# Early loads of an attention and MLP kernel, each issued when the load three places ahead has landed

## The chip, the cores and the metric

One core of a Trainium2 chip runs the whole program. The metric is the device time of one execution in microseconds (us), the median of several runs. The engines are called PE (matrix multiply, with PEld for its weight loads), DVE, ACT and POOL (elementwise engines) and SP, whose queue issues nearly all transfers. A transfer is cut over the core's 16 DMA engines and counts as landed when all its parts are there.

## What is computed

First linear attention for 8 batches of 8 heads, 576 positions and head size 64; then an MLP without activation, whose weights arrive as 64-bit floats. Cut to what matters:

```python
def phi(x):                                   # q and k, scaled by D ** -0.25
    h = x @ omega.T - (x * x).sum(-1, keepdims=True) / 2
    return exp(h - h.max(-1, keepdims=True)) / sqrt(128)
kv, z = k_p.T @ v, k_p.sum(over positions)    # per batch and head
attn  = (q_p @ kv) / (q_p @ z + 1e-6)
x     = attn as (4608, 512)
out   = ((x @ w_a) * (x @ w_b)) @ w_out       # 512 -> 1536 -> 512
```

## The kernel before

The work is a graph of about 5,000 operations. Attention goes by units (one batch, two heads): `pair` does the first ones, `shifted` the later ones; the MLP follows by batches in `moe_block` and `moe_block7`. Every matmul operand in the MLP is split into a high and a low part, so weights are converted on the chip (ACT lines 452 and 454, DVE line 456, then lines 398 and 404). The order in which the operations are emitted is a list written out by hand (`ORDER`), and the buffer slot of each tile is another one (`SLOTS`), so each engine's instruction order is fixed. The change alters neither.

A transfer is emitted by the helper `dma` (line 406), which issues on SP's queue at line 407. SP does these in order: an instruction that waits holds up all transfers behind it. A few transfers are issued elsewhere (ACT's queue brings `om`, line 428; line 960 spreads `qd`), none of them on SP's queue in the first 42 us.

The first transfers that `dma` issues, numbered from 0 as the change numbers them, with their KB:

```
 0 X   256   1 X   256   2 ident 64   3 Xe    256   4 X    512   5 nat   512
 6 X   512   7 v   330   8 nat  512   9 X     512  10 v    330  11 nat   512
12 raw 512  13 raw 512  14 raw  512  15 v     330  16 raw  512  17 raw   512
18 raw 512  19 natee 256 20 natk 256 21 v     330  22 v    330  23 X     512
24 raw 512  25 raw 512  26 natq 256  27 raw   512  28 natkk 256 29 raw   512
30 raw 512  31 natk 256
```

X holds q and k of a unit, from which PE makes the scores (line 587); nat, natee, natk and natq hold the same rows the other way round, for the sums of squares (POOL line 750, ACT lines 749 and 566, then DVE lines 752 and 571); v goes to the PE bursts of line 1040; raw is a block of 64-bit weights. Loads 0 and 1 are unit 0's X, 4, 6 and 9 those of units 1 to 3; 5, 8 and 11 are the nat of units 1 to 3; 7, 10, 15 and 21 the v of units 0 to 3; 22 and 23 belong to unit 4.

Of the kernel before, what the change touches and what calls it, by code (L numbers as in the profile page):

```python
# [196 lines left out]
    at=(  # L197
        "0123456705613412652106537451673260731742751346507163014510110101010101101010100101011010101001010101101001010101010101010101010110101010101010101010101010010101"
        "01010101010101010101010101010101010101010101"),
# [23 lines left out]
    a="101010101010101010101010",  # L223
# [132 lines left out]
def tile_attention_moe(ctx: ExitStack, tc: tile.TileContext, kqt, kqtt, kqn, kqnt, vx, omst, idn, wab, wout, out):  # L356
    nc = tc.nc
# [7 lines left out]
    def f(ap):  # L365
        return ap.bitcast(F32)

    g = Graph()
    for name, n in dict(X=2, Xw=0, natw=0, nat=2, x2=0, v=2, hk=1, hq=2, qd=1, kvz=0, sm=3, sq=3, ht=3, Xt=1, xl=0, xts=2, rd=2, x=4, xa=2, xf=2, Sa=2, Sb=2, st=0,
                        w=NF, u=NF, t=0, tst=0, wo=3, raw=2, a=2, c=0, bq=0, ghl=2, osb=0, ot=0, owr=0, og=0, ogf=0, oc=0, zs=1, z2=1, zb=2, k2=2, kl=1, dn=1, tails=0, zq=2, zx=2,  # L370
                        at=CFG["AT"], ab=2, o=4).items():
# [31 lines left out]
    def subber(o, i, hi):  # L403
        return lambda e: ENG[e].tensor_tensor(o(), i(), f(hi()), op=ALU.subtract)

    def dma(dst, src):
        return lambda e: nc.sync.dma_start(dst(), src())


    ident = fixed([P, P], F32, "ident")  # L410
# [20 lines left out]
    if CFG["IDSP"]:  # L431
        g.op({"SP": 450}, dma(lambda: ident.ap[:], lambda: idn), w=[(ident, None)], prio=-1396.5, nbytes=65536)
    else:
        g.op({"ACT": 60}, lambda e: nc.scalar.dma_start(ident.ap[:], idn), w=[(ident, None)], prio=-5000, nbytes=65536)
# [35 lines left out]
    for n, (kind, i, w) in enumerate(units):  # L470
        pr = 4000 + n * 4000 / len(units)
        more = late[:10] if n < 18 else late[:6] if n < 24 else late[:3] if n < 30 else late[:1] if n < 33 else []
        raw = g.buf("raw", [P, NW], I64 if wide else F32, f"raw{n}", more)
        src = (wab[i, w] if kind == "ab" else wout[i])
        g.op({"SP": 450}, dma(lambda raw=raw: raw.ap[:], lambda src=src: src), w=[(raw, None)], alloc=[raw], prio=pr - 600,
             nbytes=P * NW * (8 if wide else 4))
        if kind == "ab":
            hb = wab_b[i, w] = g.buf("wu"[i % 2], [P, 2, NC4, P], F32R, f"w{'ab'[w]}{i}")
            v = lambda hb, k: hb.ap[:, k].rearrange("p c f -> p (c f)")
        else:  # L480
            hb = wo_b[i] = g.buf("wo", [P, 2, E], F32R, f"wo{i}")
            v = lambda hb, k: hb.ap[:, k]
        convert(raw, lambda hb=hb, v=v: v(hb, 0), lambda hb=hb, v=v: v(hb, 1), hb, NW, pr, CFG["CONV"][0] + n * CFG["CONV"][1], n < NF)
        if kind == "o":
            db = g.buf(None, None, None, f"wod{i}")
            wo_store[i] = db
            g.op({"SP": 450}, dma(lambda i=i: wod[i], lambda hb=hb: f(hb.ap)), r=[(hb, None)], w=[(db, None)], prio=pr + 600,
                 nbytes=P * 2 * E * 4)
# [1143 lines left out]
```

## Time and profile before

| | us |
|---|---|
| median of 3 runs | 1031.1 (1031.01, 1031.1, 1032.39) |
| the profiled execution's own time | 1031.69 |
| its span, first to last instruction | 1029.7 |
| PE busy in the span | 1021.7 (99%) |
| DVE busy | 789.8 (77%) |
| ACT busy | 637.8 (62%) |

The span is what the views below divide; some 2 us lie around it. The mean granted TensorE clock is 0.999. All transfers together move 312.95 MB, 304 GB/s on average.

### The profile page before, as it was taken

What the parts mean: (1) busy time and instruction counts of PE and PEld (TensorE: products, weight loads), DVE (VectorE), ACT (ScalarE), POOL (GpSimd) and SP (SyncE); (2) the same over time, 40 slices, a digit from 0 to 9 for tenths busy, and PEclk for the clock granted to TensorE, in tenths of its full rate; (3) what the DMA queues carried; (4) which work ended last, traced back from release to release, by engine and by line L of the source; (5) the groups of instructions that cost most, each with busy time, mean ns of one, the idle gap of its engine ahead of it and who ended that gap; (6) DMA issues with size and microseconds to landing.
All of it is one profiled execution on the core that took longest, in us unless ns stands there. A gap on an engine that the chain in (4) does not pass through costs nothing.

```text
span 1029.7 us, 25658 instructions
## 1 busy us (share of the span) xinstructions
PE 1021.7 (99%) x9963; PEld 900.4 (87%) x9963; DVE 789.8 (77%) x1561; ACT 637.8 (62%) x1688; POOL 110.8 (11%) x182
## 2 busy tenths in 40 slices
PE   9999999999999999999999999999999999999998
PEld 7777777778788889888889988888888999999998
DVE  7999999999987877776767767687756467877555
ACT  7999998776676666675666556675654134344322
POOL 2012111210111111111110011111110000000000
PEclk9999999999999999999999999999999999999999
DMA  9787888998999999989898998989797888989981
GB/s 355 244 308 255 274 257 281 328 320 285 338 338 321 340 350 333 341 299 324 286 341 306 325 290 284 350 273 320 242 331 244 307 281 329 366 319 346 358 310 60
DMA packets 122185, 312.95 MB, mean 304 GB/s; under 512 B 17488, under 2 KB 39120, under 8 KB 122064
## 3 DMA queue, kind: packets, MB, share of 16 engines
q1 hardware_dynamic: 121600, 310.72, 87.6%
q8 instruction: 79, 1.29, 0.5%
q10 hardware_dynamic: 464, 0.59, 0.2%
q14 instruction: 42, 0.34, 0.1%
HBM read 254.74 MB, written 56.52 MB: 302 GB/s over the span
## 4 chain that ended last, share of the span: by engine, by line
PE 96%; DVE 3%; ACT 0%; issue 0%; DVEq 0%; ACTq 0%
PE p L1405 41%; PE o L1120 23%; PE pb L1307 6%; PE pa L1307 6%; PE o_P L1190 5%; PE pkv L906 3%; PE pm L977 2%; PE ppk L607 2%; PE ppk L587 2%; PE p L607 1%; PE p L1190 1%; DVE sm L659 1%; PE ppke L587 1%; DVE raw L456 0%; PE none L426 0%; DVE sq L752 0%
## 5 line engine op out<-in xcount | busy, mean ns | idle before, releaser
L1120 PE MATMUL o<-wo,ghl 128*128 128x512 f32 x1008 | 269.6, 397 | 0.0
L1120 PEld LDWEIGHTS o<-wo,ghl 128*128 128x128 f32 x1008 | 178.6, 188 | 35.5 <-issue 4.3
L396 ACT COPY c<-p 128x512 f32<-128x512 f32 x150 | 87.5, 583 | 182.0 <-PE p L1405 174.4
L1417 DVE TENSOR_TENSOR c<-p,c 128x512 f32<-128x512 f32 x144 | 98.7, 685 | 63.8 <-PE p L1405 36.5
L1405 PE MATMUL p<-Sa,t 128*128 128x256 f32 x1008 | 133.9, 282 | 0.0
L1405 PEld LDWEIGHTS p<-Sa,t 128*128 128x128 f32 x1008 | 126.9, 190 | 2.4 <-issue 0.3
L859 POOL TENSOR_TENSOR z<-hk 128x256 f32<-128x256 f32 x54 | 47.2, 873 | 610.5 <-ACT hk L627 356.1
L1481 DVE TENSOR_TENSOR c<-c 128x512 f32<-128x512 f32 x82 | 56.7, 696 | 46.3 <-ACT c L396 45.7
L1307 PE MATMUL pa<-x,wa 128*128 128x512 f32 x288 | 79.6, 400 | 0.0
L941 ACT ACTIVATE hq<-hq,dn 128x128 f32<-128x128 f32 x216 | 70.5, 393 | 11.9 <-DVE dn L937 11.5
L1307 PE MATMUL pb<-x,wb 128*128 128x512 f32 x288 | 77.8, 397 | 0.0
L1405 PE MATMUL p<-x,wb 128*128 128x256 f32 x504 | 73.5, 281 | 0.0
L1405 PE MATMUL p<-x,wa 128*128 128x256 f32 x504 | 73.4, 281 | 0.0
L1405 PEld LDWEIGHTS p<-x,wa 128*128 128x128 f32 x504 | 67.7, 189 | 2.9
L1405 PE MATMUL p<-Sb,bq 128*128 128x256 f32 x504 | 67.7, 283 | 0.0
L1405 PE MATMUL p<-x,t 128*128 128x256 f32 x504 | 67.5, 282 | 0.0
L1405 PEld LDWEIGHTS p<-Sb,bq 128*128 128x128 f32 x504 | 64.9, 189 | 2.9
L1405 PEld LDWEIGHTS p<-x,t 128*128 128x128 f32 x504 | 64.7, 189 | 2.9
L1405 PE MATMUL p<-Sb,t 128*128 128x256 f32 x504 | 67.0, 282 | 0.0
L1405 PEld LDWEIGHTS p<-x,wb 128*128 128x128 f32 x504 | 65.6, 189 | 0.1
L1405 PEld LDWEIGHTS p<-Sb,t 128*128 128x128 f32 x504 | 63.4, 189 | 1.4 <-ACT c L396 0.5
L1307 PEld LDWEIGHTS pb<-x,wb 128*128 128x128 f32 x288 | 53.3, 188 | 12.7 <-issue 0.9
(225 smaller groups left out, 1969.2 us busy)
## 6 DMA issues: line engine op xcount, KB each, us to landing
t<-td SPq DMA_DIRECT2D x168, 512.0 KB
wo<-wod SPq DMA_DIRECT2D x96, 512.0 KB
bq<-bd SPq DMA_DIRECT2D x84, 256.0 KB
qdr<-qd SPq DMA_DIRECT2D x108, 160.0 KB
hq<-qdr SPq DMA_DIRECT2D x27, 640.0 KB
X<-in_kqt_dram SPq DMA_DIRECT2D x30, 512.0 KB
raw<-in_wab_dram SPq DMA_DIRECT2D x24, 512.0 KB
td<-ts SPq DMA_DIRECT2D x24, 512.0 KB
```

The lines of the kernel that those rows point to most:

```text
L396: nc.scalar.copy(o(), i())
L587: nc.tensor.matmul(pps[w].ap[half, c * M:c * M + M], x()[rows, c * P + D * t:c * P + D * t + D], mo.ap[rows], start=True, stop=True)
L607: nc.tensor.matmul(flat[c // 4][w]()[half, c % 4 * M:c % 4 * M + M], x()[rows, c * P + D * t:c * P + D * t + D], om.ap[rows], start=True, ...
L859: g.op({"POOL": pool2(n)}, lambda e: nc.gpsimd.tensor_tensor(o(), a(), c(), op=ALU.add), r=r, w=w, alloc=list(al), prio=pri, deps=zload[-1 ...
L906: nc.tensor.matmul(pkv.ap[D * j + d:D * j + d + Q, 0:M], vb.ap[:, vc, d:d + Q], c(), start=(n == 0), stop=(n == 4))
L941: g.op({"ACT": 392}, lambda e, c=c, src=src: nc.scalar.activation(hq.ap[:, c], src(), AF.Copy, scale=dn.ap[:, c:c + 1]), r=[sd, (dn, None) ...
L1120: nc.tensor.matmul(po.ap[:], ghl.ap[:, gi, t * P:(t + 1) * P], wo.ap[:, wi], start=(n == 0 and i == 0), stop=(n == NF - 1 and i == 2))
L1190: nc.tensor.matmul(pb.ap[:, t], A[0](ai)[:, t * P:(t + 1) * P], W[0](wi), start=begin and t == j == 0, stop=stop and j == 2 and (t == 1 or ...
L1307: nc.tensor.matmul(pb.ap[:], wt.ap[:, wi, c], xs[c].at(xi), start=(c == 0 and i == 0), stop=(c == NC4 - 1 and i == 2))
L1405: nc.tensor.matmul(pb.ap[:, w], W[w][0](wi, c), X[0](xi, c), start=fresh and n == w == 0, stop=n == 5, skip_group_check=True)
L1417: g.op({"DVE": dve(SM)}, lambda e: nc.vector.tensor_tensor(o.ap[:, q], pb.ap[:], C[y[0]].ap[:, y[1]], op=ALU.add), r=[(pb, 0), (pb, 1), (C ...
L1481: g.op({"DVE": dve(SM)}, lambda e, c=C[k]: nc.vector.tensor_tensor(c.ap[:, :, 1], c.ap[:, :, 1], c.ap[:, :, 0], op=ALU.mult), r=part, w=pa ...
```

## The change

Every transfer that goes through `dma` is remembered in the order of issue. For numbers 6 to 29 a dependency is added on the transfer three places ahead, so that SP issues it only when that one has landed. Nothing else is altered: sizes, order, buffers and engines stay, and from number 30 on there is no added wait.

```diff
+    loads = []
+
     def dma(dst, src):
-        return lambda e: nc.sync.dma_start(dst(), src())
+
+        def go(e):
+            loads.append(nc.sync.dma_start(dst(), src()).ins)
+            n = len(loads) - 1
+            if 6 <= n < 30:
+                tc.add_manual_dep(loads[n], loads[n - 3].name, mybir.DependencyInfo(mybir.DependencyClass.Sync, mybir.DependencyReason.DATA), reason="few transfers at a time")
+        return go
```

## Rows read from the trace of the kernel before

**Rows 1.** The page's part 4: the chain that ended last, by engine.

```profile
PE 96%; DVE 3%; ACT 0%; issue 0%; DVEq 0%; ACTq 0%
```

**Rows 2.** Busy time by stretch: us, PE, PEld, DVE, ACT, POOL, PEclk, DMA share, GB/s.

```profile
6.00:30.00 24.00, 22.53 (x535) 18.89 (x528) 23.39 (x62) 21.37 (x77) 5.55 (x7) 1.00 1.03 399
6.00:42.00 36.00, 33.73 (x721) 28.12 (x714) 35.04 (x94) 31.94 (x102) 6.28 (x11) 1.00 0.87 331
46.00:1000.00 954.00, 953.88 (x8976) 841.57 (x8969) 732.84 (x1422) 593.00 (x1559) 103.20 (x162) 1.00 0.91 310
```

**Rows 3.** SP's waits from 0 to 46 us: us in total, times, longest us.

```profile
SPq L407 <- DVE sq L571: 9.1, 1, 9.1
SPq L407 <- DMA nat<-in_kqn_dram: 3.7, 3, 1.9
SPq L407 <- DMA raw<-in_wab_dram: 3.5, 4, 0.9
```

**Rows 4.** Timeline of SP, 0 to 70 us: start us, us, instruction, count.

```profile
0.75 0.87 SPq L407 DMA_DIRECT2D X<-in_kqt_dram  x2
...
9.89 1.66 SPq L407 DMA_DIRECT2D raw<-in_wab_dram  x2
...
13.91 1.60 SPq L407 DMA_DIRECT2D raw<-in_wab_dram  x2
...
17.38 0.33 SPq L407 DMA_DIRECT2D natee<-in_kqnt_dram  x1
...
19.93 2.13 SPq L407 DMA_DIRECT2D v<-in_vx_dram  x2
...
23.31 0.33 SPq L407 DMA_DIRECT2D raw<-in_wout_dram  x1
24.62 0.38 SPq L407 DMA_DIRECT2D raw<-in_wab_dram  x1
...
31.30 0.90 SPq L407 DMA_DIRECT2D raw<-in_wab_dram  x2
41.39 0.33 SPq L407 DMA_DIRECT2D natk<-in_kqn_dram  x1
```

**Rows 5.** Timeline of POOL, 0 to 45 us; in brackets the idle time before, and what ended it.

```profile
10.01 2.04 POOL L750 TENSOR_TENSOR nat<-nat 128x512 f32<-128x512 f32 x2 [4.88 <-DMA nat<-in_kqn_dram]
13.97 1.04 POOL L750 TENSOR_TENSOR nat<-nat 128x512 f32<-128x512 f32 x1 [1.92 <-DMA nat<-in_kqn_dram]
17.43 1.04 POOL L750 TENSOR_TENSOR nat<-nat 128x512 f32<-128x512 f32 x1 [2.42 <-DMA nat<-in_kqn_dram]
```

**Rows 6.** Timeline of DVE, 0 to 60 us.

```profile
3.72 0.69 DVE L643 TENSOR_TENSOR x<-X 128x512 f32<-128x512 f32 x1 [3.72 <-DMA X<-in_kqt_dram]
...
22.07 1.19 DVE L752 TENSOR_REDUCE sq<-nat 128x16 f32<-128x1024 f32 x1
```

**Rows 7.** Busy time in one short stretch; columns as in rows 2.

```profile
41.39:42.30 0.91, 0.91 (x5) 0.75 (x4) 0.91 (x2) 0.91 (x3) 0.00 (x0) 1.00 0.00 0
```

**Rows 8.** Timeline of ACT, 0 to 60 us.

```profile
5.93 0.63 ACT L642 ACTIVATE x2e<-Xe 128x512 f32<-128x512 f32 x1 [0.92 <-DMA Xe<-in_kqtt_dram]
...
25.12 0.78 ACT L454 ACTIVATE raw<-raw 128x512 int32<-128x512 uint32 x1
...
26.55 0.75 ACT L566 ACTIVATE natee<-natee 128x512 f32<-128x512 f32 x1
...
28.99 0.80 ACT L566 ACTIVATE natk<-natk 128x512 f32<-128x512 f32 x1
```

**Rows 9.** Timeline of PE: the X of unit 2, and the v bursts of units 0 and 3.

```profile
13.09 0.69 PE L1040 MATMUL pkv<-v,hk 128*64 128x66 f32 x16
...
15.68 0.32 PE L587 MATMUL ppk<-om,X 64*64 64x128 f32 x1
...
32.94 0.69 PE L1040 MATMUL pkv<-v,hk 128*64 128x66 f32 x16
```

**Rows 10.** DMA queues from 10 to 30 us: packets, MB, share of 16 engines.

```profile
q8 instruction: 4, 0.07, 1.4%
```

## The prediction

> **What bounds the kernel now.** I began with the chain that ended last: nearly all of it is PE [rows 1]. The table by stretch then shows where a delay can still start. From 46 to 1000 us PE idles 954.00 - 953.88 = 0.12 us, so whatever is lost or won before 46 us reaches the end as it is, and what happens to loads after that is not touched by the change. From 6 to 42 us, where the gated loads fly, PE idles 36.00 - 33.73 = 2.27 us, and from 6 to 30 us DVE idles only 24.00 - 23.39 = 0.61 us [rows 2]. DVE sets the pace of that stretch. From 6 to 30 us the 16 DMA engines are full too (share 1.03, 399 GB/s) [rows 2]. At that rate 512 KB take 524,288 / 399,000 = 1.31 us, 330 KB 0.85, 256 KB 0.66.
>
> Next come SP's own waits. Already now SP waits for loads: three times for a nat, four times for a raw [rows 3]. Which ones can be read by pairing. POOL is released by the nat loads 5, 8 and 11 at 10.01, 13.97 and 17.43 [rows 5]; SP issues numbers 13, 16 and 19 (the first of each raw pair, and natee) at 9.89, 13.91 and 17.38 [rows 4]. Each is eight places behind. So **the kernel already runs with a gate of eight**; the change makes it three for 24 loads. The pairing also gives landing times: a later issue stands for the landing eight places ahead. Number 16 landed at 23.31 (issue of 24) and number 17 at 24.62 (issue of 25) [rows 4].
>
> **The change, part by part.** *The waits themselves.* There are 24 new waits in SP's queue. What they hold up is only the next loads: nothing else goes through SP before 42 us. At the far end SP has 9.1 us of waiting for a buffer, for DVE, ahead of number 31 [rows 3], issued at 41.39; numbers 29 and 30 went out from 31.30 [rows 4]. Gated, 29 follows 26 and goes out some 2 us later; that is swallowed by the 9.1 us. From 31 on the queue is where it was. Cost: 0; without that cover, 2 us for number 31.
>
> *Does a gate of three still feed the DMA engines?* The order on the queue is unchanged, so a load is late only if the queue runs dry before it. Between the landing of n-3 and the landing of n the engines need the time of n-2, n-1 and n at the full rate; the gate needs the time of a lone transfer, issue to landing. No row shows a lone 512 KB load, so I bound it. Below: number 31, issued into an empty queue, has moved no byte 0.91 us later (share 0.00 from 41.39 to 42.30) [rows 7], so 0.91 + 1.31 = 2.22 us. Above: number 0, 256 KB, issued at 0.75 [rows 4], releases DVE at 3.72 [rows 6], 2.97 us with two other loads close by; plus 0.66 for the other half, 3.63 us. I take the upper end, which is a landing in fact and not a start. Three 512 KB loads need 3 x 1.31 = 3.93 us, 0.30 more than 3.63: **covered**. Two of 512 and a v need 3.47, 0.16 short where the last is a 512 and enough where it is the v (3.16). Short by more is only the run of small loads: number 20 (pace 1.31 + 0.66 + 0.66 = 2.63 against 2.97, 0.34 late), 21 (0.66 + 0.66 + 0.85 = 2.17 against 3.16, 0.99 late), and those behind it, which inherit about 1.0. At the lower end of the lone time nothing is late. A gain in landing is excluded while the order stands and the engines are full.
>
> *Who needs which load, and when.* Xe (3) landed by 5.93 [rows 8], so number 6 lands by 5.93 + 3.63 = 9.56; unit 2's X is first read at 15.68 [rows 9]. Number 4 is one 512 KB step behind Xe, 7.24; the v of unit 0 then lands by 7.24 + 3.16 = 10.40, and is read at 13.09 [rows 9]. Number 8 waits for 5: 9.89 + 3.63 = 13.52, before its 13.91 of now [rows 4]. Number 11 waits for 8: 13.91 + 3.63 = 17.54, 0.16 late against 17.38 [rows 4]; POOL idles ahead of it, works 2 x 1.04 us on it [rows 5] and the DVE sum that reads it starts at 22.07 [rows 6]: hidden by over 2 us. natee (19) has the least room: now it lands at 24.62 + 1.31 + 0.66 = 26.59 by pace, and ACT reads it at 26.55 with no idle time before [rows 8]. Gated by 16 it can land at 23.31 + 2.97 = 26.28, so it isn't late; a shortfall of 0.16 handed down from 16 still fits. natk (20) may be 0.34 late from 27.25; ACT reads it at 28.99 [rows 8]. Number 21 may be 1.0 late from 28.10; PE reads it at 32.94 [rows 9]. Raw blocks: the first is touched at 25.12 [rows 8], while number 13, a raw, landed by 19.93 (issue of 21) [rows 4]; the last raws wait for their turn far longer.
>
> The sum on the path is therefore 0, with 0 and about 0.5 us as ends (should natee inherit some of the shortfalls). The durations come from the profiled execution, whose own time is 1031.69 (span 1029.7); the three runs have their median at 1031.1, 0.6 below it, and I predict on that scale: **1031.1 us**. A difference under 0.2% (2.1 us) can't be told from no change here.
>
> **The rivals.** *Slower: the stalls of different DMA engines add up.* The gate waits for the last of 16 parts. From 10 to 30 us four instruction fetches take 1.4% of 16 engines' 20 us, 4.48 us, 1.12 us each, each on one engine [rows 10]. With eight loads queued, an engine that was stalled falls behind alone; with three, the other 15 may be left waiting, and the next stall, on another engine, comes on top. Three of the four fall before natee: 3.36 us, less the room of the rounds 7, 10, 13, 16 and 19 (four times 0.31, less 0.16), 1.1: natee 2.3 us late, ACT with it, then DVE, which has no idle time to give back: 1033.4 us. It decides if the fetches hit different engines and the lag of one exceeds the 0.3 us of room. For it: natee has no slack. Against it: the engine that is already last sets the landings of now, and it is never the one left dry. 0.14. The Trainium skill, "DMA: Bandwidth & Descriptors", section "Why a DMA increments its semaphore by 16 and not by 1", says that only the full count of 16 means that all has landed, which is this rival's premise; no row here shows the parts singly.
>
> *Faster.* If fewer queued loads let an early one land sooner, the most to be won in the stretch is PE's 2.27 us of idle time [rows 2], and its parts are not waits for loads: 1028.8 us, and by DVE's 0.61 us rather 1030.5. For it I see nothing but that a wait for nat shows on POOL [rows 5]; against it, the unchanged order. 0.04.
>
> *The change does nothing:* the added dependency is dropped as already implied, and SP still issues number 13 at 9.9 us. Eight places back does not imply three, so 0.05; 1031.1 us.
>
> **How the numbers follow.** Forecast 0.77, slower rival 0.14, does nothing 0.05, faster rival 0.04. Forecast and "nothing" both lie within 0.2%: same 0.82, slower 0.14, faster 0.04. The range runs from 1030.4 (DVE's 0.61 us all won) to 1033.4, which takes in the 0.5 us, the 1.3 us by which the highest of the three runs stands above the median, and the rival's price.
>
> **What would show it.** In the profile after: SP issues number 6 near 5.9 us, 8 near 9.9 and 9 about 1.3 us later; DMA share stays near 1.0 from 6 to 19 us and dips a little about 25 to 28; POOL's nat at 10.0, 14.0 and 17.4; ACT's natee within 0.3 us of 26.55; number 31 at 41.4. PE's idle time from 46 us on stays at some 0.1 us. I am wrong if natee starts over 1 us late, if the DMA share falls below 0.9 between 10 and 24 us, or if number 31 moves. A gain of over 2 us would mean that loads limited the first 40 us in a way that these views don't show.

## The result, and the profile after

The kernel with the gate takes 1038.43 us (median of 6 runs, 1036.59 to 1039.12); the kernel before, run beside it, takes 1031.13 us (6 runs, 1030.96 to 1032.39). The ratio is 1.0064, with a 95% interval of 1.0053 to 1.0075: slower by some 7 us, and outside the predicted range. The profiled execution took 1038.96 us with a span of 1037.1, 7.4 us more than the 1029.7 of before. Lines behind the edit have numbers higher by 8 than before (587 is now 595, 566 is 574); the helper's transfers stand at line 411.

The page's part 4, the chain that ended last by engine, now holds transfers, where before it was PE and DVE with next to nothing else [rows 1]:

```profile
PE 94%; DMA 3%; DVE 1%; ACT 0%; SPq 0%; issue 0%; ACTq 0%
```

Drawn for the first 60 us in order of time (start us, us, what), the chain shows which transfers:

```profile
2.61 5.08 DMA X<-in_kqt_dram
7.77 4.84 DMA v<-in_vx_dram
12.63 6.19 DMA v<-in_vx_dram
18.83 5.31 DMA raw<-in_wab_dram
24.16 4.74 DMA raw<-in_wab_dram
28.92 5.26 DMA natee<-in_kqnt_dram
34.20 0.63 ACT natee L574
```

These are the loads 4, 7, 10, 13, 16 and 19: every third one, each issued when the one before it in this list has landed. Five gated links last 4.74 to 6.19 us, 5.27 on average ((34.18 - 7.77) / 5 = 5.28 by landings), where the prediction had at most 3.93. The end of the chain is natee. ACT and DVE wait for it (idle time before, and what ended it, in brackets):

```profile
34.20 0.63 ACT L574 ACTIVATE natee<-natee 128x512 f32<-128x512 f32 x1 [6.47 <-DMA natee<-in_kqnt_dram]
```

```profile
34.86 0.69 DVE L579 TENSOR_REDUCE sqe<-natee 128x8 f32<-128x512 f32 x1 [6.54 <-ACT natee L574]
```

ACT read natee at 26.55 before [rows 8] and reads it at 34.20 now: 7.65 us later, and the span is 7.4 us longer. The table by stretch (columns as in rows 2) shows where it was lost and that none of it came back:

```profile
6.00:30.00 24.00, 20.14 (x473) 16.29 (x465) 21.73 (x51) 18.38 (x65) 5.56 (x7) 1.00 0.85 286
30.00:35.00 5.00, 0.02 (x2) 0.02 (x2) 0.14 (x1) 0.80 (x3) 0.00 (x0) 0.72 0.54 154
35.00:40.00 5.00, 5.00 (x58) 4.71 (x60) 4.67 (x16) 4.32 (x15) 0.00 (x0) 0.60 0.93 318
33.00:39.00 6.00, 4.02 (x48) 3.90 (x49) 4.01 (x14) 4.55 (x15) 0.00 (x0) 0.50 0.74 231
46.00:1000.00 954.00, 953.88 (x8995) 840.31 (x8996) 738.79 (x1437) 599.97 (x1575) 103.41 (x163) 1.00 0.90 310
```

From 6 to 30 us the DMA engines move 286 GB/s at a share of 0.85, against 399 at 1.03 [rows 2]. From 30 to 35 us PE works 0.02 us. From 46 us on PE idles 954.00 - 953.88 = 0.12 us, exactly as before. From 33 to 39 us the granted TensorE clock is 0.50, the lower of its two levels (1.2 and 2.4 GHz), after PE stood still from 28.99 to 34.98 us; the 0.72 and 0.60 above are means over both levels. It adds nothing that can be seen, since the span grew by 7.4 us and natee's delay is 7.65.

SP's own queue, waits from 0 to 46 us (us in total, times, longest), then its issues (start us, us):

```profile
SPq L411 <- DMA X<-in_kqt_dram: 9.0, 4, 3.7
SPq L411 <- DMA raw<-in_wab_dram: 6.6, 5, 2.2
SPq L411 <- DMA raw<-in_wout_dram: 5.8, 3, 2.3
```

```profile
6.41 0.34 SPq L411 DMA_DIRECT2D X<-in_kqt_dram  x1
7.77 0.33 SPq L411 DMA_DIRECT2D v<-in_vx_dram  x1
9.17 0.38 SPq L411 DMA_DIRECT2D nat<-in_kqn_dram  x1
11.82 0.33 SPq L411 DMA_DIRECT2D X<-in_kqt_dram  x1
...
13.91 0.38 SPq L411 DMA_DIRECT2D nat<-in_kqn_dram  x1
18.06 0.33 SPq L411 DMA_DIRECT2D raw<-in_wout_dram  x1
18.83 2.19 SPq L411 DMA_DIRECT2D raw<-in_wab_dram  x2
...
28.92 0.33 SPq L411 DMA_DIRECT2D natee<-in_kqnt_dram  x1
```

The first gated loads go nearly as forecast: 6 at 6.41, 8 at 9.17, and number 11, which waits for 8, at 13.91, just when 16 went out before by the same landing [rows 4]. Number 9 goes out 2.65 us behind 8, not 1.3, and from it on each load lands later than before. POOL shows the same: the first nat, number 5, starts there at 9.24, even 0.77 us earlier, the second still at 13.97, and the third, number 11, at 20.22 instead of 17.43 [rows 5].

```profile
9.24 2.04 POOL L758 TENSOR_TENSOR nat<-nat 128x512 f32<-128x512 f32 x2 [3.98 <-DMA nat<-in_kqn_dram]
13.97 1.04 POOL L758 TENSOR_TENSOR nat<-nat 128x512 f32<-128x512 f32 x1 [2.69 <-DMA nat<-in_kqn_dram]
20.22 1.04 POOL L758 TENSOR_TENSOR nat<-nat 128x512 f32<-128x512 f32 x1 [5.22 <-DMA nat<-in_kqn_dram]
```

Every load lands in 16 parts, one for each DMA engine. No view of the profile prints them singly, but the trace holds each landing. For some loads of both kernels (us; the first, 15th and last part to land, and the last behind the 15th):

```
            before                            after
load    first   15th   last   last-15th   issue  first   15th   last   last-15th
 4       6.15   7.42   7.52     0.10       2.61   6.47   7.63   7.69     0.06
 7       9.55  11.96  12.71     0.75       7.77  10.56  11.71  12.61     0.90
10      13.25  15.41  16.01     0.60      12.63  15.78  17.07  18.82     1.75
13      17.16  19.32  19.91     0.59      18.83  22.37  23.42  24.15     0.73
16      20.51  22.71  23.29     0.58      24.16  27.47  28.64  28.90     0.26
19      23.77  25.95  26.50     0.55      28.92  31.13  32.32  34.18     1.86
```

In before the last part lands some 2.75 us after the first for load after load (19.91 - 17.16, 23.29 - 20.51): an engine that has fallen behind seems to stay behind, and the DMA engines are full all the same (share 1.03 [rows 2]). In after the next load waits for exactly that part. On the chain, load 4 included, the last part comes 5.56 us after the fifteenth in sum, against 0.55 for natee in before; counted so, about 5.0 of natee's 7.68 us (34.18 - 26.50) sit in the sixteenth part alone.

### The profile page after: what moved, and what is told of

Read it like the earlier page. It is cut to its first block, busy times and chain, and to the rows that moved or that the text cites. A ratio compares the mean times of both kernels' runs of the same rounds, so it can differ in the third digit from the quotient of the medians.

```text
span 1037.1 us, 25661 instructions
## 1 busy us (share of the span) xinstructions
PE 1022.2 (99%) x9963; PEld 901.1 (87%) x9963; DVE 791.3 (76%) x1561; ACT 638.9 (62%) x1688; POOL 110.8 (11%) x182
## 4 chain that ended last, share of the span: by engine, by line
PE 94%; DMA 3%; DVE 1%; ACT 0%; SPq 0%; issue 0%; ACTq 0%
PE p L1413 41%; PE o L1128 23%; PE pb L1315 6%; PE pa L1315 6%; PE o_P L1198 5%; PE pkv L914 3%; PE pm L985 2%; PE ppk L615 2%; PE p L615 1%; PE ppk L595 1%; DMA v<-in_vx_dram 1%; DMA raw<-in_wab_dram 1%; PE p L1198 1%; PE ppke L595 1%; DMA natee<-in_kqnt_dram 1%; DMA X<-in_kqt_dram 0%
```

## The experiments

All kernels alter only the lines that the change added; each compares with runs of the kernel before on the same chip. Two theories stood first. **A**: a round is long in itself, a load needs about 5 us from issue to landing even alone. **B**: a load alone is as short as the prediction had it, and the rounds grow because loads in flight hold each other up (the prediction's slower rival). Later ones ask where the gate costs, and what a round consists of.

### One, two, four and five loads in flight

```diff
-                tc.add_manual_dep(loads[n], loads[n - 3].name, ...
+                tc.add_manual_dep(loads[n], loads[n - 1].name, ...
```

> Loads 6 to 29 each wait for the load directly ahead, so every gap between two issues of SP is one lone transfer, issue to landing. Theory A (the round is long by itself: a load needs about 5 us from issue to landing however few are queued): gaps of 4.5 to 5.3 us for 512 KB; load 19 (natee) lands some 14 x 4.7 = 66 us after load 5, at 75 us instead of 26.5, total about 1079 us. Theory B (a lone load needs only 3.0 to 3.6 us, and the 4.7 to 6.2 us seen with a gate of three come from waiting for the slowest of 16 engines, whose stalls add up): gaps of 3.0 to 3.2 us for 256 and 330 KB and 3.6 us for 512 KB; natee at about 58 us, total about 1063 us.

Measured: 1076.75 us (one run). SP's issues under this gate are the lone times themselves, as each load goes out when the one before it has landed:

```profile
21.09 0.33 SPq L411 DMA_DIRECT2D X<-in_kqt_dram  x1
24.52 0.33 SPq L411 DMA_DIRECT2D v<-in_vx_dram  x1
27.23 0.38 SPq L411 DMA_DIRECT2D nat<-in_kqn_dram  x1
...
49.84 0.33 SPq L411 DMA_DIRECT2D raw<-in_wout_dram  x1
53.03 0.33 SPq L411 DMA_DIRECT2D natee<-in_kqnt_dram  x1
55.67 0.33 SPq L411 DMA_DIRECT2D natk<-in_kqn_dram  x1
```

```profile
55.68 0.63 ACT L574 ACTIVATE natee<-natee 128x512 f32<-128x512 f32 x1 [16.62 <-DMA natee<-in_kqnt_dram]
```

A lone 512 KB takes 24.52 - 21.09 = 3.43 and 53.03 - 49.84 = 3.19 us, 330 KB 2.71, natee's 256 KB 2.64. **A falls**: the prediction's upper bounds of 3.63, 3.16 and 2.97 were, if anything, too high. ACT reads natee at 55.68, near B's 58. The total is nearer to A's number all the same: the span is 1074.8 us, 45.1 longer, where natee is 29.1 late. The chain that ended last goes on behind natee through the loads 22 to 26 and 28, which B's total left out.

Three lone loads are longer, and each has one 16 KB instruction fetch in it. The DMA queues (packets, MB, share of 16 engines) from 60.87 to 64.79 us, the time of one v of 330 KB:

```profile
q8 instruction: 1, 0.02, 2.3%
```

This v takes 3.92 us; v loads with none take 2.85 (40.69 to 43.54) and 2.67 (58.20 to 60.87), 1.1 to 1.25 us less. Number 7, another v, takes 3.77, and number 24, of 512 KB, 4.64 (68.25 to 72.89) against 3.19. By the landings the 16 parts of these three lie 1.4 to 1.8 us apart, those of the loads from 6 to 23 without such a fetch 0.2 to 0.65. Not every fetch does it: the one at 36.77 adds some 0.3 us to number 13, and the one at 27.10, long before the first part of number 11 lands at 30.51, shows none.

```diff
-                tc.add_manual_dep(loads[n], loads[n - 3].name, ...
+                tc.add_manual_dep(loads[n], loads[n - 2].name, ...
```

> Gate of two places. Theory A (round fixed at about 5 us): two loads per round, 2.5 us per load, natee lands at about 8 + 14 x 2.5 = 43 us, total about 1047 us. Theory B (lone round 3.0 to 3.6 us plus what stalls add): about 1.8 us per load plus the stalls, some 2.1 us with them, natee at about 37 us, total about 1042 us.

Measured: 1045.78 us (one run); ACT reads natee at 39.14. Both fall between the two theories, the total nearer A's, natee nearer B's.

```diff
-                tc.add_manual_dep(loads[n], loads[n - 3].name, ...
+                tc.add_manual_dep(loads[n], loads[n - 4].name, ...
```

> Gate of four places. Theory A: four loads per round of about 5.3 us are 1.33 us per load, nearly the full rate; natee at most 1 us late, 1031 to 1032.2 us. Theory B: the room per round grows from 0.3 to 1.6 us, more than one stall of 1.1 us; the same 1031 to 1032.2 us. Both fail if it stays over 1034.

Measured: 1033.47 us (10 runs, 1032.17 to 1034.66), ratio 1.0016 [1.0007, 1.0025]; natee read at 28.40 after a wait of 2.13 us. That is under the 1034 us at which both theories would have failed, but 1.3 us over the range that both gave.

```diff
-                tc.add_manual_dep(loads[n], loads[n - 3].name, ...
+                tc.add_manual_dep(loads[n], loads[n - 5].name, ...
```

> Gate of five places. Both theories: rounds of about 5.3 us against 5 x 1.31 = 6.6 us of queued work; no loss, 1030.9 to 1031.8 us.

Measured: 1031.34 us (1030.77 to 1033.61), ratio 1.0002 [0.9992, 1.0011]. ACT's natee in the two, first the gate of four:

```profile
28.40 0.63 ACT L574 ACTIVATE natee<-natee 128x512 f32<-128x512 f32 x1 [2.13 <-DMA natee<-in_kqnt_dram]
```

```profile
27.80 0.63 ACT L574 ACTIVATE natee<-natee 128x512 f32<-128x512 f32 x1 [0.56 <-DMA natee<-in_kqnt_dram]
```

So five in flight are enough, four nearly, three are not. The DMA rate from 6 to 30 us goes the same way: 143, 226, 286, 341 and 359 GB/s for a gate of one to five, 399 with none. From about 9.5 us, when load 5 lands, 14 loads follow to natee; a round of k loads, k times a fourteenth of the time to ACT's natee, lasts 3.3 us for one in flight, 4.2 for two, 5.3 for three, 5.4 for four ((28.40 - 9.5) / 14 x 4) and 6.5 for five. The larger of the lone time (3.2) and of k times the pace of before ((26.55 - 9.5) / 14 = 1.22) would be 3.2, 3.2, 3.7, 4.9 and 6.1. The 359 GB/s and 6.5 us of the gate of five come from an execution of 1033.61 us, 2.3 over its median, so they are rather a low and a high value. The rule holds best at the ends, where one of the two rules by far, and fails most in between, by 1.0 us for two in flight and 1.6 for three.

### Where the gate costs

```diff
-            if 6 <= n < 30:
+            if 6 <= n < 13:
```

> Gate of three for loads 6 to 12 only; 13 to 29 as before. Both theories: the lateness gathered by load 12 (its landing was 4.3 us late under the full gate: 22.88 against 18.62) can't be made up afterwards, as the DMA engines are full; natee lands about 4.3 us late and the total is about 1035 us. If lateness could be made up, or if another load than natee set the loss: 1031 to 1032 us.

Measured: 1035.35 us (1034.48 to 1036.63), ratio 1.0035 [1.0024, 1.0046]; natee read at 30.42, 3.9 us late.

```diff
-            if 6 <= n < 30:
+            if 6 <= n < 20:
```

> Gate of three for loads 6 to 19 only, natee being the last gated one. If natee is the load that sets the loss: all of it, 1036.5 to 1039 us. If the smaller loads from 20 on (natk, v, v, X) carry a share, as the prediction's run of small loads has it: at least 1 us less.

Measured: 1037.49 us (1035.9 to 1038.78), ratio 1.0062 [1.0045, 1.0079]: as much as the whole gate.

```diff
-            if 6 <= n < 30:
+            if 20 <= n < 30:
```

> Gate of three for loads 20 to 29 only. natee is ungated and lands at about 26.5; the v of unit 3 has 4.9 us of room, natk 1.8 us. At the round of 5.3 us seen under the full gate, natk (gated by 17, landing near 24.6) lands at about 29.3, 0.3 us after its use at 29.0, and the v of unit 3 at about 31.2, before 32.9: 1031 to 1031.8 us. If the gate's price doesn't hang on natee's place, this kernel loses at least 2 us: over 1033.

Measured: 1031.12 us (1030.46 to 1031.86), ratio 0.9995 [0.9986, 1.0004]. ACT's natee stands as in before, with no wait:

```profile
26.26 0.74 ACT L574 ACTIVATE natee<-natee 128x512 f32<-128x512 f32 x1
```

The three together: the whole loss is made by the gates up to natee, about half of it by the first seven (ratio 1.0035 of 1.0064), and a delay isn't made up although the later loads are free: with the first seven gated, load 12 lands 2.7 us late and natee 3.9, with the DMA engines full (share 1.01 from 18 to 30 us). The gates behind natee, where the prediction had its larger shortfalls of 0.34 and 0.99 us, cost nothing.

```diff
-            if 6 <= n < 30:
+            if 6 <= n < 30 and n % 3 == 1:
```

> Only every third load (7, 10, 13, ... 28) waits for the one three places ahead, so the loads come in bursts of three and the chain of waits that led to natee (4, 7, 10, 13, 16, 19) is kept whole. If the loss is the length of these five rounds alone, it stays: natee some 7 us late, 1036.5 to 1039 us. If each gated load pays by itself (every wait for the slowest engine lets the other engines run dry and start again), five waits in place of fourteen take more than half of it away: 1032.5 to 1034.5 us.

Measured: 1035.2 us (1034.28 to 1037.8), ratio 1.004 [1.0024, 1.0056]; natee read at 30.68. Ahead of natee this keeps just the five links of the chain shown above and drops the nine other gates. By the ratios (1.004 and 1.0064, with intervals that barely overlap) over a third of the loss goes, by natee (3.5 of 7.65 us) nearly half. So it doesn't look like this chain of five rounds alone: the gates of the loads between its links add to it. A likely reason, only argued, is that a load which they delay stands in the queue ahead of the next link.

### Finer release

Each of the first 30 loads is cut in two halves and a half waits for the one six places ahead, so that as many bytes are in flight but the release comes in smaller steps; each way of cutting has a control without an added wait (the condition then never holds).

```diff
+            for rows in (slice(0, P // 2), slice(P // 2, P)):
+                loads.append(nc.sync.dma_start(dst()[rows], src()[rows]).ins)
...
+                if 12 <= n < 60:
+                    tc.add_manual_dep(loads[n], loads[n - 6].name, ...
```

> Each of the first 30 loads is issued as two transfers of 64 partitions, and each half waits for the half six places ahead: as many bytes in flight as with three whole loads, released in smaller steps. If bytes in flight over a fixed time are what sets the pace, nothing changes: 1037 to 1039 us. If what counts is the room left while the slowest engine finishes the released piece (2.5 loads instead of 2 still queued, and a shorter lone time of about 2.6 us), this stands between a gate of three and a gate of four: 1033.5 to 1036 us.

> Control for the halves: the same two transfers per load with no added wait; what is left is the eight-place wait that the kernel always had, now eight halves, so four loads. Like the gate of four, 1032 to 1034.5 us. If the split costs something by itself, more; if the eight-place wait does not count halves as I take it, 1031 to 1031.8 us.

Measured: 1045.68 us, ratio 1.0139 [1.0124, 1.0154], and 1046.25 for the control, ratio 1.0143 [1.0124, 1.0163]. The cut by partitions costs some 15 us by itself and the gate nothing more, so the pair says nothing about the release. In the control, from 12 to 18 us (columns as in rows 2), the engines are full, yet move 241 GB/s, where 128 partitions gave 408 in the same stretch (second line, the kernel before):

```profile
12.00:18.00 6.00, 5.64 (x98) 5.32 (x102) 3.07 (x7) 0.64 (x4) 2.04 (x2) 0.50 1.05 241
12.00:18.00 6.00, 5.60 (x133) 4.30 (x126) 5.97 (x14) 5.62 (x23) 1.66 (x3) 1.00 1.03 408
```

With loads that slow, the gate of six halves seems to be covered. So the cut was made by columns instead, 128 partitions in each half:

```diff
+            half = to.shape[1] // 2
+            for cut in (slice(0, half), slice(half, 2 * half)):
+                loads.append(nc.sync.dma_start(to[:, cut], at[:, cut]).ins)
```

> Each of the first 30 loads is issued as two transfers over all 128 partitions and half the columns each, and each half waits for the half six places ahead: as many bytes in flight as with three whole loads, released in smaller steps (the split by partitions had halved the rate of each transfer, so it told nothing of this). If bytes in flight over a fixed time set the pace, nothing changes: 1037 to 1039 us. If the room left while the slowest engine finishes the released piece counts, between a gate of three and one of four: 1033.5 to 1036 us.

> Control for the halves by columns: no added wait; the eight-place wait that the kernel always had now spans eight halves, four loads. If the split is free in itself, at most the price of a gate of four, with finer steps: 1031 to 1033.5 us.

Measured: 1038.26 us (1037.62 to 1039.41), ratio 1.0065 [1.0049, 1.0082], and 1034.54 (1033.51 to 1036.54) for the control, ratio 1.0027 [1.0018, 1.0037]. The total equals that of the changed kernel; net of the cut the gate still costs 1038.26 - 1034.54 = 3.7 us. That total lies in the range expected if bytes in flight set the pace (1037 to 1039), not in the one for a finer release (1033.5 to 1036), and the control is 1 us over its own. As the cut itself takes 2.8 to 3.4 us, how much a finer release takes back isn't settled.

### Which part releases

What was left open: is a round long because the release waits for the sixteenth part, or are three loads too few whichever part gives the release? A 4-byte transfer (a marker) is put behind each of the loads 3 to 26; it runs on one engine only and queues there behind that engine's part of the load. In the first kernel a load waits for the marker three places ahead, in the second for the whole load three places ahead, in the third for nothing added (in place of 'mark' in single quotes, the second kernel has 'load' and the third an empty text).

```diff
+            if 'mark' and 6 <= n < 30:
+                to = marks[n - 3] if 'mark' == "mark" else loads[n - 3]
+                tc.add_manual_dep(loads[n], to.name, ...
+            if 3 <= n < 27:
+                marks[n] = nc.sync.dma_start(mark.ap[:, n:n + 1], idn[0:1, n:n + 1]).ins
```

> Behind each of the loads 3 to 26 the queue gets a transfer of 4 bytes (one engine's part only), and loads 6 to 29 wait for the marker of the load three places ahead instead of for that load. So the release comes from one engine, not from the last of 16. Because the eight semaphores now go round over twice as many transfers, each load also waits in full for the load four places ahead, which by the gate of four costs 1.0 to 3 us by itself. Theory 'the last part': the wait for the sixteenth part is most of the loss; 1033.0 to 1035.5, natee read by ACT before 30.5 us, and over 3 us below the kernel with the same markers and the gate on whole loads. Theory 'three loads are too few whichever part releases': 1038 to 1041, natee at 34 us or later, no different from the kernel with the gate on whole loads.

> The same markers, but loads 6 to 29 wait for the whole load three places ahead, as the changed kernel does. Both theories: 1038.4, or up to 2 us more for the markers' own packets and for 0.35 us of issue each: 1038 to 1041, natee at 34 to 36 us.

> The same markers without any added wait, to price the markers and the gate of four that the eight semaphores make of them: 1033 to 1035, natee at 28 to 30 us, by both theories.

Measured: gate on the marker 1034.07 us (1033.28 to 1035.48), ratio 1.0025 [1.0013, 1.0038]; gate on the whole load 1038.0 (1037.86 to 1039.31), ratio 1.0067 [1.0052, 1.0082]; markers alone 1034.16 (1033.22 to 1034.88), ratio 1.0027 [1.0016, 1.0038]. With the gate on the whole load ACT reads natee 2 us before the 34 us that were expected. ACT's natee in this order:

```profile
29.35 0.63 ACT L578 ACTIVATE natee<-natee 128x512 f32<-128x512 f32 x1 [2.34 <-DMA natee<-in_kqnt_dram]
```

```profile
32.01 0.63 ACT L578 ACTIVATE natee<-natee 128x512 f32<-128x512 f32 x1 [4.45 <-DMA natee<-in_kqnt_dram]
```

```profile
28.57 0.63 ACT L578 ACTIVATE natee<-natee 128x512 f32<-128x512 f32 x1 [1.92 <-DMA natee<-in_kqnt_dram]
```

The markers alone already cost 1034.16 - 1031.11 = 3.05 us; a likely part of it is that the old wait eight transfers ahead now falls four loads ahead (the gate of four by itself: ratio 1.0016). On top of that, the gate on whole loads costs 1038.0 - 1034.16 = 3.84 us, the gate on one engine's part 1034.07 - 1034.16 = -0.09, with some 1.2 us either way on each. In the profiled executions natee is read 3.44 us later than with the markers alone (32.01 - 28.57) and 0.78 later (29.35 - 28.57). That gate is no empty one: in the first kernel SP waits 18 times for a marker in the first 46 us, and its rate from 6 to 30 us is 321 GB/s against 344 for the markers alone and 287 for the gate on whole loads:

```profile
SPq L412 <- DMA mark<-in_idn_dram: 14.4, 18, 2.0
```

By the trace a load there goes out within 0.14 us of the marker's landing, and that lies 0.6 us before the last part of the marker's own load on average (loads 3 to 16, from 1.5 before it to 0.2 behind). Over five rounds that makes 3 us, an estimate, beside the 3.84 us of the medians and the 2.66 (32.01 - 29.35) of natee. So of what a gate of three costs beyond one of four, **nearly all is the wait from one engine's part to the last part**. What the gate of four costs by itself, these kernels don't take apart. The Trainium skill, "DMA: Bandwidth & Descriptors", section "Why a DMA increments its semaphore by 16 and not by 1", says that engines finish independently and that a transfer of one element uses one engine alone; the trace agrees, with 16 landings for a load and one for a marker, which shows besides it only an update some 0.45 us after its issue.

## Why the prediction was wrong

**What bounds the kernel** was right: a delay that stands at 46 us reaches the end as it is. In the profiled executions natee's delay and the growth of the span go together (7.65 and 7.4 us in after, 1.85 and 1.5 with the gate of four), as long as no later load is late as well, as under a gate of one.

**The step that failed** is "Does a gate of three still feed the DMA engines?", at the sentence that three 512 KB loads need 3.93 us, 0.30 more than a lone load's 3.63: "covered". Both numbers were good (pace 1.31, lone time 3.2 to 3.4); taking the larger of the two was not. Load n-3 counts as landed only when its slowest engine is done. By then the other engines have used up their parts of n-2 and n-1, as far as they are ahead, and stand dry until load n begins to move; it lands its lone time after its issue. The room needed is the lone time plus the distance between the first engine and the last. The rows of before hid this distance, because a queue of eight covers it; its landings show it, 2.75 us. Three times 1.31 against 3.2 + 2.75 = 5.95 us is short by 2 us in a round; 5.95 / 1.31 = 4.5 loads would have been wanted, which agrees with five being free and four not quite. This sum was made after the runs, and 2 us is more than came: the links last 5.27 us, 1.34 over 3.93. With the spread that the gated loads themselves show, 2.2 us on average over loads 6 to 19 in after, the sum gives 5.4.

**The waits themselves at the far end**, cost 0: right. Number 31 did move, to 49.44 us, but with natee's delay in front of it; with the gate only from 20 on nothing is lost.

**Who needs which load**: right that natee has the least room, that 8 holds its time, and that the small loads behind it are hidden. The shortfalls that it took to be the larger ones, 0.34 and 0.99 us, were not those that counted, and those of 0.16 ahead of natee were far too small: number 11 lands 2.8 us late, natee 7.7.

**The slower rival** named the mechanism, and its premise, that the gate waits for the last part and this costs time, is now shown by the markers; its chance of 0.14 was too low, and its price of 2.3 us was a third of what came. The term that was too small is the number and length of the delays: it counted three fetches of 1.12 us less 0.31 us of room in four rounds. There was no such room: it came from the larger-of-two rule. And of the 16 KB fetches four fell before natee, one into each of four links (first four lines; 7.77 to 12.63, 12.63 to 18.83, 18.83 to 24.16 and 28.92 to 34.20 us) and none into the link from 24.16 to 28.92 (last line):

```profile
q8 instruction: 1, 0.02, 1.3%
q8 instruction: 1, 0.02, 0.9%
q8 instruction: 1, 0.02, 2.0%
q8 instruction: 1, 0.02, 1.1%
q14 instruction: 1, 0.01, 0.4%
```

In those four the last part lags the fifteenth by 0.90, 1.75, 0.73 and 1.86 us, in the other one by 0.26. Together the four take 4.6 us of an engine by their packets, which without any room would make more than half of natee's 7.65. This is a coincidence in time, which fits the rival but doesn't show it: the link without one lasts 4.74 us all the same, and in before the parts of load 5 already land 2.43 us apart, ahead of the first 16 KB fetch at 10.58. How much of the engines' spread comes from instruction fetches, and what the rest is, stays open; it wasn't tried to take fetches away. The argument against it, that the engine already last is never left dry, may hold but is beside the point, for it is the others that stand dry (share 0.85 from 6 to 30 us).

**Faster** and **does nothing** fell: only load 5 landed clearly earlier, by 0.77 us, to no gain, and SP issues number 13 at 18.83 us, where before it went out at 9.89 [rows 4]. The signs named for being wrong (natee over 1 us late, a DMA share below 0.9, with 0.80 from 10 to 24 us, number 31 moved) all came.

## What to carry to other kernels

A limit on loads in flight has to cover the time of a lone load and the spread between the fastest and the slowest of its parts: here, by a sum made afterwards, (3.2 + 2.75) / 1.31, so five loads of 512 KB, not the three that bandwidth and lone time alone would ask for. A queue that is always full hides that spread, so a trace of a full queue doesn't show what a shorter one costs; look at single landings, or try a gate of one and read the lone times off it. Here the load with the least room before its reader carried the whole loss, and while the DMA engines were full a delay wasn't made up.

## What was not expected of the hardware

Two transfers of 64 partitions each were far slower than one of 128: 241 GB/s against 408 from 12 to 18 us with the engines as busy (share 1.05 and 1.03), and 15 us on this kernel. Cutting the same loads by columns cost 3 us. A 4-byte transfer behind each of 24 loads wasn't free either: it cost 3 us. A likely part of it, only argued, is that the transfers share eight semaphores, so that half as many loads may be under way.
